# A hand-ordered attention-and-mixer kernel with another order table: the prologue's loads reordered, two loads assumed to land later, fewer repeated score matmuls

## The chip, the cores and the metric

One core of a Trainium2 chip. The metric is device time of one execution in microseconds (us). The kernel before took 784.28, 784.71 and 784.94 us in three runs, median 784.71. The execution that was profiled took 784.66 us; 782.9 us of it is the span from the first to the last instruction of the program, so 1.8 us lie around it. On this kernel a measurement can tell about 0.2% (1.57 us) from no change.

## The reference

```python
xn = _layernorm(x)                      # x: 1 x 2048 x 640, bf16
q, k, v = heads(xn @ wqkv)              # 32 heads of 20
s = softmax(q @ k.T * 20**-0.5) @ v @ wo
h = gelu(_layernorm(xn) @ w1)           # its four quarters shifted along the sequence by +1, -1, +2, -2
x1 = xn + shifted(h) @ w2
g = silu(x1 + gelu(_layernorm(x1) @ w3) @ w4)
return x + s * g
```

## The kernel before

The attention is done in eight quads of four heads (`attn_quad`, L1374), each quad in four chunks of 512 queries (`qc`), each chunk in 16 key tiles of 128 keys. For one key tile the four heads' scores are four tiles of 128 keys by 512 queries, each in one PSUM bank. ACT takes two heads at once through exp (`exp_act`, L1692, 128 x 1024); in some key tiles it takes all four at once (L1669, 128 x 2048). For another part of the key tiles DVE turns scores into integer bits (L1714) and DVE or POOL add offsets to them (L1602, L1600), which stands for the exp. PE then multiplies by the values (L1432 for ACT's tiles, L1614 for the bits). The number of exps on ACT is fixed by a table of how many blocks go to DVE (`ND`), which the change doesn't touch.

PE makes a score in one of two ways (`score_pair`, L1625). In **row mode** (L1623) one matmul with a contraction of 32 rows makes one head's tile, and four heads stand beside each other in the four row groups of the array. In **column mode** (L1640) four matmuls over all 128 rows and 32 columns each make one tile, from a masked copy of the queries (`QM`). All other products, the projections (`mm_tile`, L733) and the value products too, are in column mode. Whether a score runs in row mode is decided from the order alone (L252): it does if PE is in row mode already, or if the next PE task is a score too. A run of row-mode tasks between two column-mode tasks is called a burst here. `AGAIN` (L585) names score tiles whose matmul is issued once or more again, to the same result.

The second branch (`b_branch`) is woven between the quads: w1 with quad 0, w2 with quad 1, w3 and w4 with quads 2 to 5. `stack` (L1279) projects queries and keys of six heads at a time, `v_load` and `v_proj` (L1335, L1344) the values of half the heads; the second half's weights are loaded with quad 1 (`ld_wv1`). `b_w4` (L2101) loads half of w4 four times (L2110). The prologue loads x in eight pieces (L920), the first query and key weights (`ld_wp_0`, `ld_wp_1`, L1102) and the first value weights (`ld_wv0`, L1341), normalises x on DVE, ACT and POOL (L944 to L1028), transposes it on PE (L1079, evicted at L1087 and L1090), and makes the first keys and queries (`KT_0`, `QT_0`); chunk 0 of quad 0 starts with an early bound (`she`, L1192, `qade`, L1196). The end is a chain of output projections (`finish_qc`, `last_half`), in which half chunks of scores are made in pairs (L1489 in row mode, L1493 in column mode).

**Nothing here is scheduled while it runs.** `program` lists 6939 tasks with what they read and write. `TABLE` (L2138), a string, names every task once, two characters each, and behind a task that takes PSUM banks or probability buffers one character for each choice of them. `follow` (L219) walks it: the order in the string is the order on each engine, and the characters fix the banks. It also reckons start times with assumed durations (L302 to L305: a DMA is taken to land after its issue, 2050 ns, its bytes at 330 a ns, and `dlat`); these times emit no instruction. `plan_sync` (L323) adds the semaphore waits that the tasks need. So PE, ACT, DVE, POOL and the DMA issues on SP each run a fixed list in order, and a task whose operand is late holds all that stand behind it.

PSUM has seven banks for scores and projections and one for the value sums. A score can only be made when the last reader of its banks is done: the exp two or three places ahead of it on ACT, or a DVE eviction.

Of the kernel before, what the change touches and what calls it, by code (L numbers as in the profile page):

```python
# [477 lines left out]
class Cfg:  # L478
# [5 lines left out]
    def __init__(self, S=2048, D=640, H=32, F=1536):  # L484
# [100 lines left out]
        self.AGAIN = {(7, 1, 2, 0): 1, (7, 1, 4, 0): 2, (7, 1, 4, 2): 2, (7, 1, 4, 3): 2, (7, 1, 6, 0): 1, (7, 1, 6, 1): 2, (7, 1, 6, 2): 1, (7, 1, 9, 0): 1, (7, 1, 9, 1): 1, (7, 1, 9, 3): 1, (7, 2, 2, 2): 4, (7, 2, 2, 3): 1}  # L585
# [71 lines left out]
class Gen:  # L657
# [677 lines left out]
    def v_load(self, hf):  # L1335
        cfg = self.cfg
        D = cfg.D
        Wv = self.alloc(f"Wv{hf}", [cfg.KC, D // 2], BF16)
        src = self.aps["A_wqkv"].rearrange("(kc p) n -> p kc n", p=128)
        c0 = 2 * D + hf * (D // 2)  # L1340
        self.T("sp", C_SP, lambda e: e.dma_start(Wv[:, :, :], src[:, :, c0:c0 + D // 2]), writes=[self.A(f"Wv{hf}")], is_dma=True,  # L1341
               nbytes=128 * D * cfg.KC, name=f"ld_wv{hf}")
# [758 lines left out]
    def b_w4(self, n0, n1):  # L2101
        cfg = self.cfg
        T, A = self.T, self.A
        D, FC = cfg.D, cfg.FC
# [3 lines left out]
        for hh in range(2):  # L2108
            hs = slice(hh * HALF, (hh + 1) * HALF)
            T("sp", C_SP, lambda e, hs=hs: e.dma_start(W4[:, :, :], w4src[:, :, hs]),  # L2110
              writes=[A("W4")], is_dma=True, nbytes=FC * 128 * D, dlat=800.0, name=f"ld_w4_{n0 // 4}_{hh}", stream="w4")
# [27 lines left out]
    r"#Z$K#6#9#:#;#<#=#>#?#@&R###%$?#w#&$4#(#,#-$S#$#A#B#C#D#E#)#F#G#H#I#J#K$L#[#]#^#a#'#*#l#_#2#L#+#.&S#e#f#c#g#h#n#p#i$T$U#`#q#m#j$N#r$V$J#o$M#k$O#s#{#t#y$P%o#M#"  # L2139
    r"N#O#P$v'#x#Q#R#|$q%#z$Q$R#u#}${(#v$W#~$#$(#S#T$|$`$}$r$)$+$Y$X$*%$#$s$t$l&#b&Q#d$~$m$w$$$Z$n$o$u$p%#%%%&%'$x#U#V%($y$,$z$[$'$]#W#X#Y%`)%a$a$%$^$5$9$_%b#/&T#%"  # L2140
    r"g&%c%d%h$-$6$.%i%e$&$b$A$C%n$8$7$/$0$2$3&U&V%)$%j%8'&j(%.%&k%k%9%=)%>$:%?%@&l%/%*%+%0%,#0%1&m%:&n%;%A&W&X%2&c)&d%l$@$D&e%3%%4&f&g%<%f%5%6&['&]%C&^&_%q$;&o&Y$"
    r"E%-%7&`%r$$1%t#%u&w(%v&x%m$c$d$B&a%s$<&y&z&{$F$=&h$G&|$>$f$e$I$g*<$*?(*;#*@)%w'()')'**=%'+&6(',&7&8&9*9$*A)'-%B%D*8#*:#&})&:&~*4(*5)%E'#'$*6&'%**#*+$*,$$h(H%"
    r"x$H$i*>%K$&;$j%Z('&%U%%V$k%p%L%F)%y%W%[%G%H%]%^%I%M%X%z#5%N#4%_%P&(K%{'%|%}%Q%R%S%~*C'%J%O%Y*1(*2)*B&*D#%T*3(#7&#&&&&'&(&)&*';#'<'='>(G&$'?&+&-&.&<(I'@*.%&%*"
    r"-&&H$&2%&I&3&J&K&L*7*`'*_(*K$*/%&,*J#*I%&M*H&*0&?$&@&A*a&&B&4#&C*M*N*L$&D&5+'#+($*R(+)%*P%*O&*E'/#'0&q$*S(*U*F'1'2'3*X$*W#'4*Y#&=%&>&r&s*Q'*[&*T*Z%&t*V&u*b(+"
    r"3$(L+2#&v(J*i'*c)&Z&0*])*h&+4$'A*G'I('J'K'L*l'M*^3$*k+T+$$+%#*d('N+&)*o'*m%*n&*r*p('5$*s'6'7'8'9':*e+6#&E*v*q#(P+5$'B#+*+7&*f&+C(*g%*j)+D)'C'D'E'F'O&'U''V'W'"
# [135 lines left out]
```

## Time and profile before

| | us |
|---|---|
| median of three runs | 784.71 |
| profiled execution, whole | 784.66 |
| its span | 782.9 |
| PE, ACT, DVE, POOL busy | 771.1, 764.3, 700.4, 440.7 |
| exps of 128 x 1024 on ACT: count, summed busy time | 730, 677.1 |
| score matmuls in row mode: count | 1907 |
| score matmuls in column mode: count | 384 |

A line of the timeline reads: start in us, duration in us, engine, line of the kernel, operation, what is written <- what is read, how many were merged, and in brackets the idle time of the engine before it and what ended that. An instruction's end includes the time in which its pipeline drains, and the next one of the same engine starts inside it: in an unbroken run the exps start about 0.9 us apart, though one is shown as 1.02 us or longer.

### The profile page before, as it was taken

Reading aid. Unit: us, or ns where it says so; the run is one execution under the profiler, and the core shown is the slowest. Engines: PE = TensorE matmul, PEld = TensorE weight load, DVE = VectorE, ACT = ScalarE, POOL = GpSimd, SP = SyncE. Lnnn points to the kernel's source line nnn. Section 1 sums busy time; section 2 is a strip of 40 time slices with the busy share of each in tenths; the row PEclk is TensorE's granted clock in tenths of the full one; section 3 lists DMA queues with packets and bytes.
Section 4 is the critical chain, followed back from the end, with each engine's and each line's share of the span. In section 5 each row is a group of like instructions: output and inputs, shape, how many; then the busy total and the mean of one; then the engine's idle time right before and its main releaser. Section 6 shows DMA issues by size and latency. Waiting matters only on the chain.

```text
span 782.9 us, 28034 instructions
## 1 busy us (share of the span) xinstructions
PE 771.1 (98%) x12501; PEld 294.9 (38%) x12501; DVE 700.4 (89%) x1170; ACT 764.3 (98%) x803; POOL 440.7 (56%) x238
## 2 busy tenths in 40 slices
PE   8999999999999999999999999999999999999997
PEld 4433333335434322333433344333235333333554
DVE  7889899988999999997989889998989888898886
ACT  7999999999999999999999999999999999999996
POOL 5676646545257656566554654666454555636743
PEclk9999999999999999999999999999999999999999
DMA  5333442423131323623223341234431133114433
GB/s 173 34 111 76 108 110 67 102 79 70 28 72 21 57 66 72 134 55 66 46 62 74 67 93 35 65 59 85 103 70 23 32 55 81 19 19 136 106 119 120
DMA packets 141352, 58.12 MB, mean 74 GB/s; under 512 B 113728, under 2 KB 136432, under 8 KB 141232
## 3 DMA queue, kind: packets, MB, share of 16 engines
q1 hardware_dynamic: 141232, 56.33, 31.6%
q8 instruction: 98, 1.61, 0.9%
q14 instruction: 22, 0.18, 0.1%
HBM read 34.70 MB, written 10.33 MB: 58 GB/s over the span
## 4 chain that ended last, share of the span: by engine, by line
PE 59%; ACT 38%; DVE 1%; SPq 1%; DMA 1%; issue 0%
ACT arena L1692 33%; PE psum L733 22%; PE psum L1623 16%; PE psum L1614 9%; PE psum L1432 7%; ACT arena L2095 3%; PE psum L1640 2%; ACT arena L1669 1%; DMA arena<-in_A_wqkv_dram 1%; ACT arena L2123 1%; SPq L920 1%; PE psum L1489 1%; PE psum L1463 0%; PE psum L1493 0%; ACT L1692 0%; ACT L2095 0%
## 5 line engine op out<-in xcount | busy, mean ns | idle before, releaser
L1692 ACT ACTIVATE arena<-psum 128x1024 bf16<-128x1024 f32 x730 | 677.1, 1105 | 6.2 <-PE psum L1623 3.7
L1600 POOL TENSOR_TENSOR arena<-arena 128x2048 int32<-128x2048 int32 x92 | 330.2, 3598 | 197.1 <-DVE arena L1602 88.7
L1714 DVE TENSOR_SCALAR arena<-psum 128x512 uint16<-128x512 f32 x528 | 341.5, 683 | 39.1 <-PE psum L1623 31.1
L733 PE MATMUL psum<-arena 128*32 128x320 bf16 (+1 forms) x5808 | 335.0, 333 | 0.5 <-DMA arena<-in_A_wqkv_dram 0.5
L1623 PE MATMUL psum<-arena 32*128 32x512 bf16 x1907 | 252.3, 384 | 3.0 <-ACT arena L1692 1.8
L1614 PE MATMUL psum<-arena 128*22 128x512 bf16 x2112 | 183.6, 381 | 0.0
L733 PEld LDWEIGHTS psum<-arena 128*32 128x32 bf16 x5808 | 137.9, 96 | 120.6 <-issue 48.2
L1623 PEld LDWEIGHTS psum<-arena 32*128 32x128 bf16 x1907 | 69.0, 91 | 221.7 <-ACT arena L1692 114.4
L1432 PE MATMUL psum<-arena 128*22 128x512 bf16 x1456 | 139.3, 382 | 0.1
L1602 DVE TENSOR_SCALAR arena<-arena 128x4096 uint16<-128x4096 uint16 (+1 forms) x121 | 131.9, 1106 | 1.6 <-PE psum L1614 0.6
L1746 POOL TENSOR_TENSOR arena<-arena 128x512 bf16<-128x512 f32 x30 | 40.6, 1354 | 55.3 <-DVE arena L1602 41.9
L1614 PEld LDWEIGHTS psum<-arena 128*22 128x22 bf16 x2112 | 47.1, 90 | 60.7 <-issue 42.8
L1432 PEld LDWEIGHTS psum<-arena 128*22 128x22 bf16 x1456 | 35.5, 90 | 45.7 <-issue 31.2
L1640 PE MATMUL psum<-arena 128*32 128x512 bf16 x384 | 37.6, 382 | 0.0
L2088 DVE CAST arena<-psum 128x512 bf16<-128x512 f32 x48 | 32.7, 682 | 3.5 <-PE psum L733 3.3
L1299 DVE CAST arena<-psum 128x512 bf16<-128x512 f32 x40 | 27.2, 683 | 6.0 <-PE psum L733 5.7
L1911 POOL TENSOR_TENSOR arena<-arena 128x640 bf16<-128x640 bf16 x12 | 16.7, 1399 | 19.4 <-DVE arena L1845 11.1
L1669 ACT ACTIVATE arena<-psum 128x2048 bf16<-128x2048 f32 x13 | 25.2, 1941 | 0.5 <-PE psum L1623 0.5
L944 DVE BATCH_NORM_STATS2 arena<-arena 128x6 f32<-128x320 bf16 x54 | 24.1, 476 | 1.3 <-DMA arena<-in_A_x_dram 1.1
L1845 DVE SCALAR_TENSOR_TENSOR arena<-psum,arena 128x320 bf16<-128x320 f32 x32 | 15.6, 489 | 8.1 <-PE psum L733 7.7
L1733 DVE STREAM_TRANSPOSE arena<-psum 128x512 f32<-128x512 f32 x30 | 21.3, 710 | 1.2 <-PE psum L1432 0.8
L2095 ACT ACTIVATE arena<-arena 128x6144 bf16<-128x6144 bf16 x4 | 21.1, 5316 | 0.0
(135 smaller groups left out, 331.6 us busy)
## 6 DMA issues: line engine op xcount, KB each, us to landing
arena<-in_B_w_dram SPq DMA_DIRECT2D x48, 160.0 KB, 2.7
arena<-arena SPq DMA_DIRECT2D x124, 32.0 KB, 1.9
arena<-in_B_w_dram SPq DMA_DIRECT2D x4, 960.0 KB, 5.4
arena<-in_A_x_dram SPq DMA_DIRECT2D x8, 320.0 KB, 6.4
arena<-in_A_x_dram SPq DMA_DIRECT2D x16, 160.0 KB, 2.5
out_dram<-arena SPq DMA_DIRECT2D x16, 160.0 KB, 2.3
heads<-arena SPq DMA_DIRECT2D x120, 20.0 KB, 2.0
arena<-queries SPq DMA_DIRECT2D x28, 80.0 KB
```

The source lines that it names most:

```text
L733: ins = e.matmul(pb[32 * c:32 * c + 32, 0:N], lhsT(k, c), rhs(k, c), start=(k == 0), stop=(stop and k == nk - 1), tile_position=(0, 32 * c))
L1432: ins = e.matmul(pb[32 * i:32 * i + 22, 0:512], VA[:, ql, kts[i // 2], i, :], PT[:, slots[i // 2][0].slot, slots[i // 2][0].at(i % 2):slot ...
L1600: return e.tensor_tensor(dst.bitcast(I32), U[:, ub, 0:w].bitcast(I32), bass.AP(c.tensor, c.offset, [list(c.ap[0]), [0, w // 2]]), op=ALU.add)
L1602: fa if onp else lambda e, v=v, dst=dst: e.tensor_scalar(dst, U[:, ub, 0:w], EXP_B[v], None, op0=ALU.add),
L1614: ins = e.matmul(pb[32 * i:32 * i + 22, 0:512], wv, dst[:, at:at + 512].bitcast(BF16), start=first, stop=final, tile_position=(0, 32 * i))
L1623: return e.matmul(out, self.KT[32 * i:32 * i + 32, b, 128 * kt:128 * kt + 128], q, start=True, stop=True, tile_position=(32 * i, 0))
L1640: ins = e.matmul(out[32 * c:32 * c + 32, :], self.KT[:, b, 128 * kt + 32 * c:128 * kt + 32 * c + 32], self.QM[:, gb, i, :], start=True, st ...
L1669: lambda e: e.activation(self.PT[:, hp[0].slot:hp[0].slot + 2, :], self.psum[:, 512 * h0.slot:512 * h0.slot + 2048].rearrange("p (a b) -> ...
L1692: lambda e: e.activation(self.PT[:, hp.slot, :].rearrange("p (a b) -> p a b", b=512), self.banks(hs), AF.Exp, scale=cfg.scale),
L1714: T("dve", c_dve(512), lambda e, h=h, y=y: e.tensor_scalar(U[:, ub, y:y + 512], self.bank(h.slot)[:, :], a_exp, EXP_BIAS, op0=ALU.mult, op ...
L1746: return e.tensor_tensor(OnT.rearrange("p (k d a) -> p a k d", k=4, a=4), Ob[:, :].rearrange("p (a k d) -> p a k d", a=4, k=4), in1, op=AL ...
L2095: T("act", c_act(FC * 512), lambda e, G=G, i=i: e.activation(G[:, i, :, :], G[:, i, :, :], AF.Gelu_apprx_tanh), reads=gta, writes=gta, nam ...
```

## The change

- **TABLE** is another string: the same 6939 tasks in another order with other banks. Read task by task, ACT keeps 704 of 786 tasks at their place and moves none by more than 4; PE keeps 805 of 4466 and moves some by up to 123; DVE keeps 300 of 1170, POOL 104 of 234, SP 82 of 283.
- **AGAIN** goes from 12 tiles with 19 extra matmuls (all in chunks 1 and 2 of the last quad) to 5 tiles with 6 (one of them in quad 3).
- **dlat**, the assumed extra time to landing, goes from 800 to 2000 ns for w4 and from 0 to 1200 ns for the second value weights. These enter only the planner's arithmetic.

The prologue's loads are issued in this order (the number is the first x tile of a piece of two):

```
before: x0 x2 x4 x6 x12 x8 wp_1 x10 x14 wv0 wp_0
after:  x0 x2 x4 x6 x10 wp_1 x8 x14 x12 wp_0 wv0
```

Of ACT's list up to the first exp, both hold the same 23 tasks; the eviction of the first queries (`qev_0`) changes place with a Square pass over x (`ln1a_14_sxx14`) that stood behind it. On PE, `KT_0_0` comes ahead of the first `QT_0`, and one more task, `KT_1_3`, stands before the first burst.

Counted over both orders:

| | before | after |
|---|---|---|
| row-mode bursts on PE | 567 | 581 |
| summed depth of the bursts (matmuls of the fullest row group, repeats included) | 655 | 665 |
| score tiles in column mode (four 512-column matmuls each) | 96 | 82 |
| half-chunk pairs in column mode (16 matmuls each) | 6 | 8 |
| exps that take a bank freed by the exp right ahead of them | 2 | 2 |

The two of the last row are, before, the wide exp of key tile 8 in chunk 3 of quad 2 and an exp of key tile 6 in chunk 1 of quad 5; after, an exp of key tile 4 in chunk 0 of quad 1 and one of key tile 12 in chunk 2 of quad 7. Besides, an exp of the prologue (`exp0_0_3_1`) gets its banks from the eviction right ahead of it.

```diff
-        self.AGAIN = {(7, 1, 2, 0): 1, (7, 1, 4, 0): 2, (7, 1, 4, 2): 2, (7, 1, 4, 3): 2, (7, 1, 6, 0): 1, (7, 1, 6, 1): 2, (7, 1, 6, 2): 1, (7, 1, 9, 0): 1, (7, 1, 9, 1): 1, (7, 1, 9, 3): 1, (7, 2, 2, 2): 4, (7, 2, 2, 3): 1}
+        self.AGAIN = {(3, 1, 10, 2): 1, (7, 1, 2, 1): 1, (7, 1, 6, 2): 1, (7, 1, 12, 1): 2, (7, 1, 15, 0): 1}
...
-               nbytes=128 * D * cfg.KC, name=f"ld_wv{hf}")
+               nbytes=128 * D * cfg.KC, dlat=1200.0 * hf, name=f"ld_wv{hf}")
...
-              writes=[A("W4")], is_dma=True, nbytes=FC * 128 * D, dlat=800.0, name=f"ld_w4_{n0 // 4}_{hh}", stream="w4")
+              writes=[A("W4")], is_dma=True, nbytes=FC * 128 * D, dlat=2000.0, name=f"ld_w4_{n0 // 4}_{hh}", stream="w4")
...
 TABLE = (
...
```

More of the change, by code (lines that the diff above doesn't have):

```diff
@@ L2142 @@
[L2142 to L2145, printed above, removed]
@@ new lines @@
+    r"#&w)%C$0$@&o$B%u%v%w&x&y&Y$c$E%s$1$<$?$F$>&h&z%m&{*?#$d*<)&|*;(*@$*A%%x'(($G')*='%B'*$e$='+',&6)&7*9#*8$$f$I$g*:&$h'-&8&9&}($H*5(*4)&~*6(%E%D&:'#**#*+$'$'%$i"
+    r"$j%U%$k*,$%y%F$%V%G%H%W%o&;%K)%z(H*>%L'&%M%P(%Q%N%I%Z&%O%[%X%R%]%^%{'%|%S%J%}*C)%T%Y*B(%_*2&*1'%~&#(I&&(&'&(&)&<&*'d*D)*-(*3&&$&+*.)*/'&-#0';&'<'=&.'>'?&H#&I"
+    r"&2)&J&K(G(J&L*7*0&,'@&3&%*_&*`%*a$*J$*K#*H(&M*I)*L'*M&?#&@&A*N(L#4'A3$&B&C&4(&D*Q&+'$(K&5+(#*E*P(*T*O)&=(*F'/)&N+)&&>'0'1*S#&q#*W#*X$'2'3*Y(&r&s*R%*[(*Z)&t&u"
+    r"*V'4*U*])&v+2$+3#*h%*i&*l+4#*k*b(*c)'I#'J'K'L'M*G*d%'N+%#+$$*^*o&*n'*p%+&'*m(*s'5$'6'7'8'9*q)'.+5$*r+6#+T'e+7(&/':*e+**g&+C(*f%+D'*j$'U$'V'W'X'B&+E%'C'D'Y'E'"
@@ new lines @@
+    r"F+<%+=&'O''P'Q'R'S+.'+/(&E*v'G+9#+#'Z']$+>&'T+:$+X&+0'+W%+;$+8'^'_+Z+,'++('`'a*x+_#+K%+[+`$+J&+-#+?'b+c&F$+H(#7+G'+1*u+V$+b+L)+U%+o&&G&O&*w,+)*y+I$(P+n'+r'''"
+    r"H*|,*(+Y#*t*{,,(&P+M+q,.&+u$,-%+x,/&+v#+y+|*z+A'+^(+])*~*},K$+@&,J%+a)'f&'g,#+B$'h'i'j+h('l$+F'k,L'+i''m'n+N,:&+j%+f$&0,;%,>+e#'o+d,=+s(+t''p'q+g$,0,A%,D,9#,"
+    r"8$,B&,E+k+w)'r$+m(,<&+l'+p(+O-.'s't,@%,G$,H#,I$,?&&i'u'v'w+P'x#'y,C%'z'{'|'},N$,O#,W(,Z,X),P#+~,M(Q,w&,x%&p,&,),`',R$,_(,[,Q#,F'c#8'[3%+Q05(M$,c,y',b(N,p&,s%"
+    r",S)'~,q'+z+{,t$->)-?(,',r&,u(-@$+},T,e,(,~&-2#-#%-1$(#,5',$-5-4,v,%,i-$#,4((%$(&(',]&,6&,1#,2$,^%,f((()(+#(,,3),a((-(.,{#(*-8(,z$-;,7,g-&%-%&(O(R-9),k-<,|%,d"
@@ new lines @@
+    r"-H(-K,U#,V$-'&,l,}(/(0-G)-J,Y)-0&-/%-3%-(($,h-M(-L'-N#-O$-R,j,o,n-P#-k%-j&(1$-Q-U(2-6'-l)-E$-7(-F#.`(Y(a-:((3(4-I',m-)(7((5(8(6-A(-B'(9-=-p&-C&-g#.%)-s-h$(:("
+    r";-_.$((<-i%-X-*.&#-D(Z#-x&-c$(=-w%+R-[-d#-{-z-e$([(](^-u)06-v((_(`-y&-m.1&-q%-~#-}$-W-V-t.((.2'.)).#)-Z(S(.4.*%-a$.5-`#(T(U.+'.8(.;-b'.9).,&.'(V.<(v(W(X.?-n$"
+    r"-o#.-(-f-]/8'-r)/9&./(.0).3'(>../:((w((x(y.7#.6$.:%-Y&1(z-T({-^.I&.>+S.B-S.M#.L$(|.J#(@-|&b.H(?(.N)(A(B.A.D.d(.S'.E.T&.U'.c).=.K.g.P%.O$.Q$0I&.f0J.j(.m.V'.k)"
+    r".W&0K.X%.n0L0M.h%.i$.l&.b(.@0N.y&.|/k'/n.a).R.Y.G.q#(E.p$.z%.}.F-+/$&.e#(C(D.s(/%'/(.r).t).C.u'/'.Z07(08.~#/#$09.w'/E(/F)/H/&%/I.x&0:0;.{$0<)(-,(}(F/*.o/5#/6"
```

200 lines of the change are left out of this document (96 added, 104 removed).

## The prediction, as it stood before the result

> **What bounds the kernel now.** I read the page first: busy shares, the chain that ended last, the costliest groups.
>
> ```profile
> PE 771.1 (98%) x12501; PEld 294.9 (38%) x12501; DVE 700.4 (89%) x1170; ACT 764.3 (98%) x803; POOL 440.7 (56%) x238
> ...
> PE 59%; ACT 38%; DVE 1%; SPq 1%; DMA 1%; issue 0%
> ...
> L1692 ACT ACTIVATE arena<-psum 128x1024 bf16<-128x1024 f32 x730 | 677.1, 1105 | 6.2 <-PE psum L1623 3.7
> L733 PE MATMUL psum<-arena 128*32 128x320 bf16 (+1 forms) x5808 | 335.0, 333 | 0.5 <-DMA arena<-in_A_wqkv_dram 0.5
> ```
>
> PE and ACT are both full, and the chain goes back and forth between them. ACT's work is fixed (730 exps and the rest), so the time can only fall by ACT's idle 782.9 - 764.3 = 18.6 us, and by gaps too short for that count. The stretches show where it lies.
>
> ```profile
> 0.00:20.00 20.00, 17.21 (x408) 9.77 (x412) 15.88 (x65) 14.62 (x29) 11.62 (x37) 1.00 0.64 173
> 20.00:40.00 20.00, 19.99 (x407) 9.06 (x398) 17.18 (x44) 18.86 (x26) 12.58 (x18) 1.00 0.21 30
> 740.00:760.00 20.00, 19.93 (x454) 10.74 (x449) 17.41 (x30) 18.80 (x21) 9.39 (x6) 1.00 0.50 152
> 760.00:783.00 23.00, 17.05 (x476) 10.99 (x468) 16.87 (x33) 15.96 (x18) 8.34 (x6) 0.92 0.35 110
> ```
>
> The columns are the stretch, its length, then busy time of PE, weight loads, DVE, ACT, POOL, the granted clock, DMA. ACT is idle 5.4 + 1.1 us in the first 40 us and 1.2 + 7.0 us in the last 43, in all 14.7 of 18.6; the 700 us between hold 3.9. PE looks full, but its score weight loads mostly wait for a bank:
>
> ```profile
> PEld psum L1623 <- ACT arena L1692: 114.4, 304, 0.7
> ```
>
> So 304 of 567 bursts start when ACT frees a bank, after 0.38 us on average. The middle is a tight loop: ACT frees a bank, PE makes the next score, ACT takes it.
>
> **The longer landings: nothing.** The group of L733 above says that projections on PE idled 0.5 us in all, for one cause, wqkv in the prologue. The loads of w4:
>
> ```profile
> L2110 SPq DMA_DIRECT2D arena<-in_B_w_dram x4: 383/408/527, 401.4 to 648.5; - x4
> its engine sat idle before it (us, times) until:
> who waited for it (us, times):
> busy tenths in 40 slices 0000000000000000000000000000000000000000
> DMA to landing us min/median/max: 5.2/5.4/6.0
> ```
>
> The planner assumed 480 + 2050 + 983040 bytes/330 + 800 ns = 6.3 us from issue, and they landed in 5.2 to 6.0; nobody waited for one. The new 7.5 us only keeps users of w4 further behind. Value taken: 0; bounds 0 to -0.3 (a wait of the size of the 0.5 us above that another execution may hold).
>
> **The prologue: -0.35 us.**
>
> ```profile
> 6.41 1.41 SPq L1341
> 7.81 0.04 issue
> 7.86 6.11 DMA arena<-in_A_wqkv_dram
> 13.96 0.14 issue
> 14.10 2.32 PE psum L733 x44
> ```
>
> This is the chain that ended last, at its start: SP issues `ld_wv0` (1.41 us), then `ld_wp_0`, whose landing at 13.96 lets PE begin `QT_0`. The change puts `ld_wp_0` ahead, so it is issued some 1.4 us earlier (the wv0 issue is what stands between). The next limit is close:
>
> ```profile
> 12.76 0.82 PE L907 MATMUL psum<-arena 128*32 128x512 bf16 x12
> 14.10 0.83 PE L733 MATMUL psum<-arena 128*32 128x512 bf16 x12 [0.52 <-DMA arena<-in_A_wqkv_dram]
> ```
>
> And ACT's own line in the same stretch:
>
> ```profile
> 11.96 1.63 ACT L1087 ACTIVATE arena<-psum 128x512 bf16<-128x512 bf16 x3
> ...
> 16.40 0.72 ACT L992 ACTIVATE arena<-arena 128x640 bf16<-128x640 bf16 x1
> ...
> 17.63 2.62 ACT L1087 ACTIVATE arena<-psum 128x512 bf16<-128x512 bf16 x5 [0.41 <-PE psum L1079]
> ...
> 22.40 1.92 ACT L1692 ACTIVATE arena<-psum 128x1024 bf16<-128x1024 f32 x2
> ...
> 29.27 1.02 ACT L1692 ACTIVATE arena<-psum 128x1024 bf16<-128x1024 f32 x1 [0.74 <-PE psum L1623]
> ```
>
> The warm-up matmuls end at 13.58 and ACT's three evictions of transposed x at 13.59, so PE can start 0.5 us earlier, no more. One more task (`KT_1_3`, 0.21 us) then stands ahead of the first scores: 0.5 - 0.2 = 0.3. ACT does the same 23 tasks before its first exp (22.40) and can save at most the 0.41 us gap at 17.63 and some tenths at its other waits. I take -0.35. Bounds: -0.7 (gap and 0.3 of PE), and +0.1, because `qev_0` now waits behind a 0.72 us Square pass, and the bound that the first scores need hangs on it; this is the cost if the earlier PE doesn't cover it. Wv0 lands later by its neighbour's issue, and its first users move back in PE's list too: 0.
>
> **PE's work: +2.9 us, of which 0.8 shows.** Two places of PE's timeline and one group of instructions give the prices.
>
> ```profile
> 511.24 0.60 PE L733 MATMUL psum<-arena 128*32 128x512 bf16 x8
> 511.67 0.39 PE L1432 MATMUL psum<-arena 128*22 128x512 bf16 x4
> 511.99 0.61 PE L1623 MATMUL psum<-arena 32*128 32x512 bf16 x6
> 512.53 0.40 PE L1614 MATMUL psum<-arena 128*22 128x512 bf16 x4
> ...
> 24.01 0.39 PE L1623 MATMUL psum<-arena 32*128 32x512 bf16 x2
> 24.33 0.67 PE L733 MATMUL psum<-arena 128*32 128x320 bf16 x12
> ```
>
> ```profile
> L1493 PE MATMUL psum<-arena 128*32 128x256 bf16 x96 | 3.7, 273 | 0.0
> ```
>
> Two column tasks of 512 columns take 511.67 - 511.24 = 0.43, so 0.215 each. The same kind of task ahead of a burst takes 511.99 - 511.67 = 0.32: entering costs 0.105. A burst one deep lasts 24.33 - 24.01 = 0.32, two deep 512.53 - 511.99 = 0.54: about 0.215 for each depth and 0.105 for leaving. A half-chunk pair in column mode is 3.7/6 = 0.62, less the 0.18 by which a shown end outlasts the start of the next (0.40 - 0.215): 0.44. From the counts in the section on the change: 14 more bursts x 0.21 = +2.9; 10 more of depth x 0.215 = +2.1 (13 fewer repeats are in it); 14 fewer column scores x 0.215 = -3.0; 2 more column pairs x 0.44 = +0.9. Sum +2.9 us. The Trainium skill, page "TensorEngine Tiling (Array Packing)", section Key Properties, says that changing the tiling mode drains TensorE; this trace agrees, with 0.105 us at each edge, and by that rule alone, with no wait to hide them, the 28 further changes of mode cost all their 2.9 us.
>
> What hides it: the wait for a bank. Of 567 bursts 304 (54%) wait 0.38 us for ACT, more than a burst's 0.21 overhead, so 46% of 2.9 = 1.35 is uncovered; and PE carries 59% of the chain: 0.8. Bounds: 0 (all in waits) to +2.9 (all on the chain).
>
> **Banks: -1.1 us.** Where an exp takes the bank of the exp right ahead of it, ACT must stand still while PE makes the score. Before there are two such exps, at 298.12 and 512.51.
>
> ```profile
> 293.78 3.84 ACT L1692 ACTIVATE arena<-psum 128x1024 bf16<-128x1024 f32 x4
> 298.12 1.88 ACT L1669 ACTIVATE arena<-psum 128x2048 bf16<-128x2048 f32 x1 [0.50 <-PE psum L1623]
> ...
> 512.51 1.94 ACT L1692 ACTIVATE arena<-psum 128x1024 bf16<-128x1024 f32 x2 [0.59 <-PE psum L1623]
> ...
> 118.38 2.98 ACT L1692 ACTIVATE arena<-psum 128x1024 bf16<-128x1024 f32 x3 [0.36 <-PE psum L1623]
> ...
> 746.25 5.08 ACT L1692 ACTIVATE arena<-psum 128x1024 bf16<-128x1024 f32 x5 [0.55 <-PE psum L1489]
> ```
>
> One exp takes 1.02 (the row of 29.27), two in a row 1.94, so they overlap by 0.1, and each stall costs its idle time plus 0.1: 0.6 + 0.7 = 1.3 us. Both exps get banks freed earlier in the new order. The new order has two others, but where ACT stood still already: behind the wide exp at 116 (now 0.36 + 0.1; a full stall of 0.65 adds 0.2) and at 746 (0.55 + 0.1; adds nothing). The prologue's exp behind an eviction stands still now too (0.74 at 29.27). Net -1.1; bounds -1.3 and, if PE is late there for other reasons, 0. The other stalls of the middle have an exp's width of slack in both orders, and the number of such exps is alike; new ones I can't see, and I give them 0 with +-1.0, a bit less than the two just priced.
>
> **The end: 0.** Behind the score of key tile 2 in the last quad's third chunk 3 fewer bursts follow (-0.6), 2 more column pairs (+0.9), and about 0.3 us of column tasks moved ahead of it: 0, bounds +-0.5. Behind the pair at 762.6 the list is the same but for its inner order, so the last 20 us stay. The pairs are part of the +2.9 and not added again. The repeats that go are counted in the depth.
>
> **Sum.** 784.66 (the profiled execution) - 0.35 + 0.8 - 1.1 = 784.0; it stands 0.05 under the median of the runs, so the median is forecast at **784.0**, -0.1%.
>
> **The rivals.**
> - *Late bursts (slower).* The 14 further bursts stand where PE, not ACT, is late; each delays an exp that ACT can't make up, since it has no spare time in the middle (3.9 us idle in 700). Price: all 2.9 on the chain and the banks' gain lost to PE being late there too: 784.66 - 0.35 + 2.9 = 787.2. It decides once more than half of 2.9 (1.57 us) is on the chain with no gain from banks. For it: PE carries 59% of the chain. Against it: 304 waits for ACT. The Trainium skill's rule of the drain (page "TensorEngine Tiling (Array Packing)", section Key Properties) would give this one too.
> - *Covered (faster).* All 2.9 us fall in the 114 us of waits, and prologue and banks give their whole: 784.66 - 0.7 - 1.3 = 782.7; with stalls of the middle falling out well (-1.0) 781.7. Taken at 782.4. For it: the two stalls are plain in the trace.
> - *The change doesn't do what it says.* Nobody waits for w4 or wv1 now, the prologue's gain is lost at `qev_0`, and the rest cancels: 784.7.
>
> **How the numbers follow.** Forecast 0.36, no effect 0.08, covered 0.31, late bursts 0.25. The forecast's own range is 783.2 to 786.2: the terms' bounds partly cancel. Same (within 0.2%): 0.36 + 0.08 = 0.44; faster 0.31, slower 0.25; 0.2% is about what a measurement of this kernel can tell from no change. The range reaches to 781.2 and 788.0: below, the covered case with the middle's 1.0 and the tail's 0.5 (784.66 - 0.7 - 1.3 - 1.0 - 0.5 = 781.2); above, the late bursts with the middle's 1.0 of new stalls (787.2 + 1.0 = 788.2, less a little). About 1 in 10 is left out on each side.
>
> **What would show it.** Right: in the prologue PE starts L733 near 13.6 with no wait for in_A_wqkv, and the first exp near 22.05; no ACT gap of over 0.4 us at the old places 298 and 512; ACT idle in the middle within 1 us of 3.9; 1908 row-mode and 328 column-mode score matmuls; PE idle or waiting less by some 2 us while the span hardly moves. Wrong: waits on w4, ACT gaps before L1623 bursts in new places with more than 2 us in all, or a first exp later than 22.5.

## The result, and the profile after

| | before | after |
|---|---|---|
| median, 7 runs each on one chip (us) | 784.70 (784.28 to 784.94) | 781.94 (781.32 to 782.75) |
| ratio of after to before | | 0.9967, 95% interval 0.9956 to 0.9979 |
| profiled execution, whole (its span) | 784.66 (782.9) | 782.75 (780.9) |

After is faster by 2.76 us or 0.33%, more than the 0.2% that can be told from no change. The forecast was 784.0 and no difference. That did not come: the median lies below the forecast's own range (783.2 to 786.2), inside the wide one (781.2 to 788.0) and near the time of the rival "covered" (782.4). The profiled execution of after is the slowest of its seven, 0.8 us above their median, so its trace shows 1.9 us of the 2.8; most of the rest is in the prologue, which differs from one execution to the next (below).

The page of after, its rows for the engines, the chain that ended last and the groups of the exps, the projections and the two kinds of score:

```profile
PE 770.5 (99%) x12470; PEld 291.4 (37%) x12470; DVE 698.9 (89%) x1170; ACT 763.0 (98%) x803; POOL 441.4 (57%) x238
...
PE 57%; ACT 40%; DVE 1%; DMA 1%; issue 0%; POOL 0%; SPq 0%
...
L1692 ACT ACTIVATE arena<-psum 128x1024 bf16<-128x1024 f32 x730 | 676.7, 1106 | 6.6 <-PE psum L1623 4.0
...
L733 PE MATMUL psum<-arena 128*32 128x320 bf16 (+1 forms) x5808 | 331.6, 333 | 0.8 <-POOL arena L1911 0.7
L1623 PE MATMUL psum<-arena 32*128 32x512 bf16 x1908 | 254.3, 384 | 1.6 <-ACT arena L1692 0.6
...
L1640 PE MATMUL psum<-arena 128*32 128x512 bf16 x328 | 32.1, 381 | 0.0
```

The same engines are full and the chain goes on between the same two. The only wait of L733's matmuls that was left before, for a DMA of wqkv, is gone; 0.7 us for GpSimd has come. The score weight loads wait for a bank freed by an exp as often and as long, though there are 14 more bursts:

```profile
PEld psum L1623 <- ACT arena L1692: 113.3, 304, 0.7
```

The first two and the last two stretches of after (columns as before):

```profile
0.00:20.00 20.00, 17.97 (x420) 9.54 (x424) 16.37 (x67) 15.18 (x30) 11.92 (x37) 1.00 0.59 174
20.00:40.00 20.00, 19.93 (x410) 8.90 (x406) 17.73 (x44) 18.82 (x26) 12.32 (x16) 1.00 0.23 36
740.00:760.00 20.00, 19.33 (x468) 10.91 (x460) 17.68 (x28) 17.94 (x20) 8.89 (x5) 1.00 0.42 121
760.00:781.00 21.00, 15.10 (x452) 10.50 (x440) 13.43 (x30) 13.85 (x15) 6.99 (x5) 0.95 0.32 106
```

ACT is busy 0.56 us more in the first 20 us than before, and 0.86 us less from 740 to 760 (17.94 against 18.80). Those are a gain and a loss at the two ends, and both have a plain cause in the traces. Between 40 and 740 us ACT's idle time fell from 3.9 to 2.7 us (17.9 us in all, less 6.0 and 9.2 at the ends).

**How the lead grows.** ACT's list holds 786 tasks in nearly the same order in both kernels, so the start of its n-th task in the one, less that in the other, is the lead at that place. The waits for the activation table are rows that stand by themselves in ACT's timeline and make good milestones; the last row is the last eviction of the kernel. Before:

```profile
183.13 1.28 ACT L2003 ACT_TABLE_LOAD   x1
...
378.59 1.28 ACT L2095 ACT_TABLE_LOAD   x1
...
587.49 1.28 ACT L2095 ACT_TABLE_LOAD   x1
...
778.71 0.70 ACT L1863 ACTIVATE arena<-psum 128x640 bf16<-128x640 f32 x1 [2.77 <-PE psum L1857]
```

After:

```profile
181.39 1.28 ACT L2003 ACT_TABLE_LOAD   x1
...
376.26 1.28 ACT L2095 ACT_TABLE_LOAD   x1
...
584.92 1.28 ACT L2095 ACT_TABLE_LOAD   x1
...
776.70 0.70 ACT L1863 ACTIVATE arena<-psum 128x640 bf16<-128x640 f32 x1 [2.78 <-PE psum L1857]
```

So after leads by 1.74, 2.33, 2.57 and 2.01 us. Task by task the lead is 0.53 us at the first exp, 0.97 at 42 us, 0.84 at 49 us, and then it grows in steps: 0.5 around 123 us, 0.4 at 168, 0.6 from 290 to 378. It is 2.48 at 498 us, 2.78 at 750 us, and 0.7 is lost at 757. Steps of 0.1 to 0.2 us that go back again stand between, also where no exp has a gap in front of it, so a step of that size says little by itself.

**The prologue.** The chain of after at its start, and ACT there:

```profile
11.53 1.57 ACT arena L1087 x3
...
13.14 0.40 PE psum L733 x4
...
13.55 1.70 PE psum L733 x28
```

```profile
21.87 4.69 ACT L1692 ACTIVATE arena<-psum 128x1024 bf16<-128x1024 f32 x5
...
28.25 1.94 ACT L1692 ACTIVATE arena<-psum 128x1024 bf16<-128x1024 f32 x2 [0.55 <-PE psum L1623]
```

PE starts the projections at 13.14 instead of 14.10, with the one key task `KT_0_0`, when ACT's third eviction is done (13.10); the queries follow at 13.55, as soon as their weights are there (landed at 13.51). The exp that stood at 29.27 before stands at 28.25.

**The stalls.** ACT's rows around the four places that the prediction priced:

```profile
115.16 1.93 ACT L1669 ACTIVATE arena<-psum 128x2048 bf16<-128x2048 f32 x1
117.64 7.51 ACT L1692 ACTIVATE arena<-psum 128x1024 bf16<-128x1024 f32 x8 [0.55 <-PE psum L1623]
...
295.56 2.02 ACT L1669 ACTIVATE arena<-psum 128x2048 bf16<-128x2048 f32 x1
297.31 4.84 ACT L1692 ACTIVATE arena<-psum 128x1024 bf16<-128x1024 f32 x5
...
507.83 1.94 ACT L1692 ACTIVATE arena<-psum 128x1024 bf16<-128x1024 f32 x2 [0.26 <-PE psum L1623]
510.02 4.69 ACT L1692 ACTIVATE arena<-psum 128x1024 bf16<-128x1024 f32 x5 [0.25 <-PE psum L1623]
...
757.10 5.61 ACT L1692 ACTIVATE arena<-psum 128x1024 bf16<-128x1024 f32 x6 [1.28 <-PE psum L1489]
```

The wide exp of 298 has no gap in front of it any more. Behind the wide exp at 115 the gap is 0.55 where it was 0.36, as the prediction had it, but the eight exps behind it run without a break, while before had another gap four exps later (0.48). Before, that exp and PE's burst for it:

```profile
122.75 3.77 ACT L1692 ACTIVATE arena<-psum 128x1024 bf16<-128x1024 f32 x4 [0.48 <-PE psum L1623]
...
122.11 0.60 PE L1623 MATMUL psum<-arena 32*128 32x512 bf16 x6
```

After, the bursts that make the same scores:

```profile
120.80 0.40 PE L1623 MATMUL psum<-arena 32*128 32x512 bf16 x4
...
121.67 0.39 PE L1623 MATMUL psum<-arena 32*128 32x512 bf16 x2
```

The orders tell what was changed. Before, the burst is two deep, and one of the two scores that the exp needs (`exp1_0_6_0`) stands in its row group behind a score for VectorE. After, that exp and the next one (`exp1_0_7_1`) change places, the scores come in two bursts one deep each, and both exps start without a gap (121.29 and 122.21).

At 510 a gap of 0.59 became 0.25, but gaps of 0.19 and 0.26 ahead of it (500 and 508 us) are new, and the lead is 2.48 at 498 us and 2.49 behind the four. The gap at 757 is 1.28 where the same exp had 0.46 before (759.06).

### The profile page after: what moved, and what is told of

The parts are those of the page before. It is cut to its first block, busy times and chain, and to the rows that moved or that the text cites. A ratio compares the mean times of both kernels' runs of the same rounds, so it can differ in the third digit from the quotient of the medians.

```text
span 780.9 us, 27979 instructions
## 1 busy us (share of the span) xinstructions
PE 770.5 (99%) x12470; PEld 291.4 (37%) x12470; DVE 698.9 (89%) x1170; ACT 763.0 (98%) x803; POOL 441.4 (57%) x238
## 4 chain that ended last, share of the span: by engine, by line
PE 57%; ACT 40%; DVE 1%; DMA 1%; issue 0%; POOL 0%; SPq 0%
ACT arena L1692 35%; PE psum L733 21%; PE psum L1623 16%; PE psum L1614 10%; PE psum L1432 7%; PE psum L1640 1%; ACT arena L2095 1%; ACT arena L1669 1%; ACT arena L2003 1%; DMA arena<-in_A_x_dram 1%; ACT arena L2123 1%; PE psum L1489 1%; PE psum L1463 1%; PE psum L1493 0%; ACT L1692 0%; PE psum L1079 0%
## 5 line engine op out<-in xcount | busy, mean ns | idle before, releaser
L733 PE MATMUL psum<-arena 128*32 128x320 bf16 (+1 forms) x5808 | 331.6, 333 | 0.8 <-POOL arena L1911 0.7
L733 PEld LDWEIGHTS psum<-arena 128*32 128x32 bf16 x5808 | 135.6, 96 | 121.1 <-issue 48.6
L1602 DVE TENSOR_SCALAR arena<-arena 128x4096 uint16<-128x4096 uint16 (+1 forms) x121 | 130.3, 1091 | 2.6 <-PE psum L1614 1.2
L1640 PE MATMUL psum<-arena 128*32 128x512 bf16 x328 | 32.1, 381 | 0.0
L1733 DVE STREAM_TRANSPOSE arena<-psum 128x512 f32<-128x512 f32 x30 | 21.3, 710 | 2.1 <-PE psum L1623 0.9
L2117 DVE TENSOR_TENSOR arena<-psum,arena 128x320 bf16<-128x320 f32 x32 | 15.6, 486 | 6.8 <-PE psum L733 6.6
```

Of the source, the lines that this page charges most:

```text
L733: ins = e.matmul(pb[32 * c:32 * c + 32, 0:N], lhsT(k, c), rhs(k, c), start=(k == 0), stop=(stop and k == nk - 1), tile_position=(0, 32 * c))
L1602: fa if onp else lambda e, v=v, dst=dst: e.tensor_scalar(dst, U[:, ub, 0:w], EXP_B[v], None, op0=ALU.add),
L1640: ins = e.matmul(out[32 * c:32 * c + 32, :], self.KT[:, b, 128 * kt + 32 * c:128 * kt + 32 * c + 32], self.QM[:, gb, i, :], start=True, st ...
```

## The experiments

The order string can be cut where the same set of tasks is done in both kernels and the same PSUM banks are held; before's part on one side and after's part on the other then make a legal third order, called a graft below (where only the buffers of the exps differ at the cut, they are renamed on one side). The cuts lie at about 49, 264, 498 and 730 us. All leads below are by ACT's tasks in one profiled execution against the profile of before, given at before's times. Each median stands beside that of before on the same chip.

**The whole prologue, first cut.**

```diff
 TABLE
-    before's order up to 49 us
+    after's order up to 49 us
     before's order from 49 us
```

> Before, with the order of after up to a seam at about 49 us (loads, prologue, first scores, and what follows them), and before's own order and banks from there on. Theory (the gain is a sum of local gains of order and banks): all of the prologue's gain stays, about 0.9 us, so 783.8 us where before stands at 784.7, and ACT runs 0.8 to 1.0 us ahead from 45 us to the end. Rival (the waits behind the seam eat it): 784.4 to 784.7, with the lead gone by about 125 us. Rival (the prologue is the whole gain and the rest only keeps it): 781.9.

796.53 us (before 785.07), ratio 1.0140 (1.0126 to 1.0155). Neither theory: ACT stands still for 12 us, and SyncE's and the chain's rows say for what.

```profile
60.10 1.02 ACT L1692 ACTIVATE arena<-psum 128x1024 bf16<-128x1024 f32 x1 [11.88 <-PE psum L1623]
```

```profile
SPq L1390 <- POOL arena L1410: 30.1, 1, 30.1
```

```profile
50.37 3.46 POOL arena L1410
...
53.85 0.64 SPq L1390
...
55.78 1.88 DMA arena<-arena
```

Read backwards: the exp waits for a score, the score for DMAs of L1390 that SyncE issues at 53.85, SyncE for a memset of GpSimd (L1410). The memset is late because the planner ties each GpSimd task to the last task of VectorE ahead of it *in the string* that takes the lock which the two share there (`lock`, L255). At the cut 19 GpSimd tasks and loads had come to stand behind VectorE's last tasks of the first part. It is a fault of the cut, no part of the change, but it prices a late GpSimd task: ACT goes from 1.0 us ahead at 42 us to 11.7 behind by 100 us, and stays 11.7 behind to 750 us.

**The old prologue in after.**

```diff
 TABLE
-    after's order up to 49 us
+    before's order up to 49 us
     after's order from 49 us
```

> After, with the order of before up to the seam at about 49 us. Theory (sum of local gains): after less the prologue's share, 782.8 to 783.0 us where after stands at 781.9. Rival (the prologue's gain is eaten by later waits): 781.9 to 782.2. Rival (the prologue is all): 784.7.

796.55 us, ratio 1.0143 (1.0130 to 1.0156): the same fault, an ACT stall of 10.8 us at 49 us, so nothing on the change.

**Fewer repeats alone.**

```diff
-        self.AGAIN = {(7, 1, 2, 0): 1, (7, 1, 4, 0): 2, (7, 1, 4, 2): 2, (7, 1, 4, 3): 2, ...
+        self.AGAIN = {(3, 1, 10, 2): 1, (7, 1, 2, 1): 1, (7, 1, 6, 2): 1, (7, 1, 12, 1): 2, (7, 1, 15, 0): 1}
```

> Before, its tables as they are, with only after's list of repeated score tiles: 10 repeats fewer, 2.2 us less of score matmuls by 0.215 us each. Theory (PE's work lies in its waits for ACT, so less of it is worth nothing): 784.5 to 784.7 us. Rival (fewer repeats are where the gain comes from): 782.0 to 782.5. If the share of PE in the chain decides (59 per cent): 783.4.

785.62 us (before 785.07), ratio 1.0006 (0.9996 to 1.0017). The expectation miscounted: the lists hold 19 and 6 extra matmuls, so 13 fewer are left, 2.8 us of PE's work; one entry is in both, so 18 go and 5 come. By the clock it is worth nothing, and the trace tells the two kinds apart. The 18 that go, all in the last quad, win ACT nothing: PE stands idle in their place (0.33 us for ACT at 716.87). The ones that come cost: ACT is 0.14 us ahead up to 334 us, where the repeat in quad 3 stands, and 0.06 behind from there; two column-mode repeats at 719 us put a gap of 0.23 in front of the next exp, and past 720 us ACT is 0.29 behind. The change's gain does not come from them.

**More repeats in the middle.** One score tile in a one-deep burst of each chunk of the quads 0 to 6 but the first is made twice (before's list, and 27 entries more):

```diff
+        (0, 1, 11, 2): 1, (0, 2, 11, 1): 1, (0, 3, 5, 2): 1, (1, 0, 14, 0): 1, (1, 1, 5, 1): 1, ...
```

> Before, with 27 score tiles more computed twice, one in a one-deep burst of each chunk of the quads 0 to 6: 27 x 0.215 = 5.8 us more of score matmuls, and not an instruction in another place. Hidden altogether: 784.7 us. The price that my prediction took (0.8 shown of 2.9, 27 per cent): 786.3. By PE's share of the chain (59 per cent): 788.1. All shown: 790.5.

788.57 us (before 785.07), ratio 1.0045 (1.0032 to 1.0058): 3.5 us of 5.8 or 60% (by the interval 43 to 78%), near what PE's share of the chain says (788.1) and more than twice what the prediction reckoned (786.3). The profile agrees by another way: the prologue of that execution was late by 2.6 us, and between 42 us and the end ACT falls back by 3.1 us more, 53%, in one step of 0.7 us near 268 us, steps of 0.1 to 0.2 us at other places and none at many of the 27.

**The prologue with the cut mended.** As the first kernel, but GpSimd's 19 tasks and loads behind the cut stand as early beside VectorE's tasks as in the kernel that they are from.

> Before, with the order of after up to a seam at about 49 us and before's own order and banks from there on. It is the first prologue kernel again with its seam mended: GpSimd's 19 instructions and loads that stood behind the seam stand again at their old places beside VectorE's, so that the 11 us stall at 47 us goes. Theory (the gain is a sum of local gains): the prologue's 0.9 us stay, ratio to before 0.9988, ACT 0.8 to 1.0 us ahead from 45 us to the end. Rival (waits behind the seam eat it): ratio 0.9996 to 1, the lead gone by about 125 us. Rival (the prologue is the whole gain): 0.9967.

783.54 us (before 784.78), ratio 0.9981 (0.9972 to 0.9990): 1.24 us. The milestones of its ACT:

```profile
181.87 1.28 ACT L2003 ACT_TABLE_LOAD   x1
...
377.33 1.28 ACT L2095 ACT_TABLE_LOAD   x1
...
586.22 1.28 ACT L2095 ACT_TABLE_LOAD   x1
...
777.46 0.70 ACT L1863 ACTIVATE arena<-psum 128x640 bf16<-128x640 f32 x1 [2.77 <-PE psum L1857]
```

A lead of 1.26, 1.26, 1.27 and 1.25 us: what the first 49 us win is still there at the end, within 0.02 us, and the medians differ by 1.24. The rival that later waits eat it is refuted; the rival that the prologue is all, as well.

**The old prologue in after, mended in the same way.**

> After, with the order of before up to the seam at about 49 us, mended in the same way. Theory (sum of local gains): after less the prologue's share, ratio to before 0.9979, ACT level with before at 45 us and 1.8 us ahead at 740 us. Rival (the prologue's gain is eaten later): 0.9967. Rival (the prologue is all): 1.0.

791.63 us, ratio 1.0084 (1.0067 to 1.0102). The mending does not suffice here: ACT still stands 5.9 us at 50.6 us behind the same memset, which the chain shows released by VectorE at 46.8 us only; after's order puts it behind VectorE's task there, and before's prologue brings that later. So "after without its prologue" was not measured.

**The loads alone.** Only SyncE's order of the first fifteen issues:

```diff
-x0 x2 x4 x6 x12 x8 wp_1 x10 x14 wv0 wp_0
+x0 x2 x4 x6 x10 wp_1 x8 x14 x12 wp_0 wv0
```

> Before, with only SyncE's order of the first fifteen issues taken from after (wp_1 behind the tenth x tile, wp_0 and wv0 last); every other engine keeps its order. If the loads are the prologue's gain: the first KT projection starts at 13.6 us or before where before's first projection starts at 14.1, the first exp at 21.9 instead of 22.4, ratio 0.9990 to 0.9994. If the order of PE's instructions is needed as well: before's first projection is of QT and waits for wp_0, the last to land at 13.5 us, so first exp 22.3 to 22.9 and ratio 1.0 to 1.0006.

784.58 us (before 784.78), ratio 0.9995 (0.9986 to 1.0004): by medians -0.2 us, and not told from nothing. In its profiled execution, which was its fastest (784.11), PE starts the projections at 12.88 us, without a wait for the weights, the first exp is at 21.44, and ACT leads by 0.74 from 28 us to 750 us. In that execution the first x tiles were ready as early as in the mended kernel (ACT's sixth task 0.76 and 0.73 us ahead of before's profile); there the lead was 1.27. So, profile against profile, the loads gave 0.74 of 1.27 us with these landings, and the order of the tasks the other 0.5; but this profile is of its kernel's fastest execution. By the medians the loads gave 0.2 and the order of the tasks 1.0. How the prologue's gain divides between the two is not settled.

**After with before's end.**

```diff
 TABLE
     after's order up to 730 us
-    after's order from 730 us
+    before's order from 730 us, buffers of the exps dealt out anew
```

> After up to a seam at about 730 us, with before's order, banks and repeats from there on (the buffers of the exponentials are dealt out anew behind the seam). After's longest new stall, 1.47 us of ACT at 754.7 us, should be before's 0.66 again. Sum of local gains: 2.6 to 2.8 us ahead of before at 740 us and to the end, ratio 0.9966, level with after or up to 0.8 us faster. Rival (after's tail is part of its gain): 0.9975 to 0.998, slower than after by 0.6 to 1 us.

783.06 us (before 784.78), ratio 0.9972 (0.9962 to 0.9983): 1.7 us faster than before, where after is 2.8. The lead is 2.8 us up to 726 us, 2.2 from 730 us and 1.6 from 751 us to the end. The new stall did not show that after's end is bad as a whole; the graft lost more than it saved. Whether before's order or the buffers dealt out anew lost it stays open.

**After up to 264 us, before from there.**

> After up to a seam at about 264 us, before's order, banks and repeats from there on. Theory (local gains that add up, none of them eaten): ACT 1.8 us ahead of before at 264 us as in after, and just as far ahead at 770 us; ratio 0.9977. Rival (the gain of one stretch is lost in the waits of the next): the lead shrinks behind the seam to 0.9 us or less, ratio 0.999.

782.92 us (before 784.74), ratio 0.9977 (0.9967 to 0.9987): as the sum of local gains has it. ACT leads by 0.96 at 49 us, 1.96 at 262 us, and by these milestones to the end:

```profile
376.63 1.28 ACT L2095 ACT_TABLE_LOAD   x1
...
585.53 1.28 ACT L2095 ACT_TABLE_LOAD   x1
...
776.74 0.70 ACT L1863 ACTIVATE arena<-psum 128x640 bf16<-128x640 f32 x1 [2.77 <-PE psum L1857]
```

1.96, 1.96 and 1.97. So after's stretch from 49 to 264 us is worth 1.00 us, as it is in both profiles of after.

**After's order from 264 to 498 us alone, in before.**

> Before, with after's order and banks between two seams at about 264 and 498 us alone. In that stretch after gains 0.65 us on before, 0.6 of it at the stall of the wide exp at 298 us. Theory (local, additive): ACT level with before up to 264 us, 0.65 us ahead from 320 us to the end, ratio 0.9992. Rival (the gain needs what after does ahead of 264 us): 1.0.

784.34 us (before 784.74), ratio 0.9999 (0.9990 to 1.0007): too small for the clock, but the trace shows it. ACT is 0.57 us behind before up to 262 us (a late prologue), 0.17 us *ahead* at 301 us, and 0.16 behind again at 498; behind the cut it keeps 0.24 to 750 us. The gap at 298 is gone and gave 0.79 us, but other stalls took back 0.46. Net 0.41 at the second cut and 0.33 behind it. In after itself the same stretch gives 0.64, in both profiles. The difference arises at 355 us, where PE waits 0.17 us for a VectorE transpose (L1733) that it does not wait for in after, and ACT loses 0.28. So the theory of purely local gains holds here only in part.

**After's order from 498 us alone, in before.**

> Before up to a seam at about 498 us, and after's order, banks and repeats from there on. In that stretch after gains 0.4 us at 511 us and loses 0.8 at 754.7 us, and its end is 0.5 us worse than its lead at 740 us. Theory (local, additive): 0.3 us ahead of before at 740 us, 0.3 to 0.5 us behind at 770 us, ratio 1.0004 to 1.0006. Rival (after's tail is a gain, as the graft of before's tail at 730 us would have it): ratio 0.9990 to 0.9994.

784.17 us (before 784.74), ratio 0.9996 (0.9987 to 1.0005). The profile: 3.23 us behind at 498 us (a late prologue once more), 2.96 at 531, but 3.2 again from 545 to 700, 3.00 at 750 and 2.97 at the end. So after's order from 498 us on is worth 0.26 us here, in steps too small to place. The gap at 757 is only 0.47 us here (0.46 before, 1.28 after), and two rows per kernel tell why. After, GpSimd's timeline and the line of the loads of x for the residual (L1835; the last number is the time from issue to landing), issued at 750.41:

```profile
754.56 1.39 POOL L1911 TENSOR_TENSOR arena<-arena 128x640 bf16<-128x640 bf16 x1 [2.10 <-DVE arena L1740]
```

```profile
L1835 SPq DMA_DIRECT2D arena<-in_A_x_dram x1: 327/327/327, 750.4 to 750.4; - x1
...
DMA to landing us min/median/max: 4.0/4.0/4.0
```

After's end in before, issued at 756.19:

```profile
759.53 1.40 POOL L1911 TENSOR_TENSOR arena<-arena 128x640 bf16<-128x640 bf16 x1 [1.28 <-DVE arena L1539]
```

```profile
L1835 SPq DMA_DIRECT2D arena<-in_A_x_dram x1: 328/328/328, 756.2 to 756.2; - x1
...
DMA to landing us min/median/max: 3.2/3.2/3.2
```

The trace names VectorE as releaser, and two different lines of it, done 0.3 us and longer before. GpSimd started 0.12 and 0.13 us behind the landing (750.41 + 4.03 = 754.44, 756.19 + 3.22 = 759.40): what it waited for was the load. The load took 0.81 us longer in after, and the gap on ACT is 0.81 us longer. Between them stands PE, which waits for that GpSimd task ahead of the score that ACT needs:

```profile
756.01 0.73 PE L733 MATMUL psum<-arena 128*32 128x320 bf16 x16 [0.67 <-POOL arena L1911]
```

**After once more, unchanged.**

> After once more, unchanged, for a second profile and a second median. Its first profiled execution took 782.75 us, the slowest of its seven, and holds a stall of ACT of 1.47 us at 754.7 us; before with after's tail from 498 us on does not show that stall. If it belongs to that one execution: no stall over 0.8 us at that place, ACT 2.6 to 3.0 us ahead of before at 770 us as at 740 us, a profiled time of 781.7 to 782.2 us. If it belongs to after's order: a stall of 1.3 to 1.6 us there again, and 782.6 to 782.9 us. First exp at 21.4 to 21.9 us as in the other kernels with after's loads; ratio 0.9956 to 0.9979 as before.

781.96 us (before 784.92), ratio 0.9966 (0.9952 to 0.9980). Both expectations fail in part. (Their 1.47 us counts from start to start of the two exps, less the 0.9 us of an unbroken run; the row's gap is 1.28.) The stall is there again (a gap of 1.13 us, 1.32 by that count; the load took 3.9 us), so it is no accident of one execution, though its length follows the load's landing; yet the profiled execution took 781.96, because its prologue was 0.6 us earlier, with the first exp at 21.24 us, earlier than expected. The lead is 3.40 at 752 us and 2.79 at the end.

## Why the prediction was right or wrong

**The sum of the parts.** What ACT's lead gains in each stretch, by the two profiles of after and by the kernels that hold the stretch without the rest of after behind it (for the last three, without the rest ahead of it too):

| stretch (us) | after | after again | in a third order |
|---|---|---|---|
| to 49 | 0.84 | 1.47 | 1.27 (mended prologue) |
| 49 to 264 | 1.00 | 1.00 | 1.00 (after up to 264) |
| 264 to 498 | 0.64 | 0.64 | 0.41 |
| 498 to 750 | 0.30 | 0.29 | 0.23 |
| 750 to the end | -0.77 | -0.62 | 0.03 |
| sum | 2.01 | 2.79 | |

By the clock the first row is 1.24 and the first two together 1.82 (1.97 in that trace); the rows below them are read from traces alone. So the change has no one cause: it is a prologue that starts earlier and many small gains in the middle, and one loss at the end. Against the forecast's -0.65, of which -0.35 is prologue and -0.3 middle, the prologue gave 0.9 more (by the clock), the middle from 49 to 498 us 1.3 more, and the end took back 0.6 to 0.8 where nothing was reckoned.

- **What bounds the kernel:** right. PE and ACT by turns, the middle a tight loop, in which a lead won on ACT is kept (1.26 us for 600 us).
- **The longer landings, 0:** right. The two `dlat` values by themselves change no instruction of any engine, and nobody waits for a load of w4 or of the second value weights in either trace. The loads of w4 in after:

```profile
L2110 SPq DMA_DIRECT2D arena<-in_B_w_dram x4: 373/406/527, 398.9 to 644.8; - x4
its engine sat idle before it (us, times) until:
who waited for it (us, times):
...
DMA to landing us min/median/max: 5.2/5.5/5.7
```

- **The prologue, -0.35 (-0.7 to +0.1):** right about what stood in the way, the query weights, but too small by 0.9 and outside its bound of -0.7. It gave the new order of the tasks nothing or a cost; that order gave 0.5 us profile against profile, 1.0 by the medians. And "so PE can start 0.5 us earlier, no more" failed: the limits that it named, ACT's evictions at 13.59 and the warm-up matmuls at 13.58, moved too (13.10 and 13.07 in after), since they depend on when the x tiles land (the chain of after goes back to a DMA of x that lands at 8.10). And the limit was one draw of a wide lot:

| first projection / first exp (us) | |
|---|---|
| before's loads, seven profiles | 14.10 / 22.40, 13.85 / 22.14, 13.93 / 22.27, 14.68 / 22.98, 15.03 / 25.02, 15.11 / 23.41, 15.66 / 25.64 |
| after's loads, seven profiles | 13.14 / 21.87, 12.70 / 21.24, 12.88 / 21.44, 12.92 / 21.46, 13.20 / 21.73, 13.21 / 21.75, 13.26 / 21.79 |

  The two latest of the first row are from the slowest executions of their kernels (790.42 and 787.63 us), so the usual spread is smaller.

The latest of the first row is PE's row in the kernel with after's end:

```profile
15.66 1.94 PE L733 MATMUL psum<-arena 128*32 128x512 bf16 x25 [2.08 <-DVE arena L973]
```

  The trace names VectorE, but in all seven the first projection starts 0.13 to 0.14 us behind the landing of the query weights, whatever engine is named (in before 13.96 and 14.10, as the prediction's chain shows; here 15.53 and 15.66). Issued at 7.86 in before and at 7.9 here, they took 6.1 us to land there and 7.6 here. In before they are the last in the list, behind wv0, and set the start every time; in after they stand ahead of wv0, one key task that does not need them goes first, and in six of the seven they were there by 12.55, before PE came to them.
- **PE's work, +2.9 of which 0.8 shows:** the share was wrong. The prediction multiplied 46% (bursts that do not wait) by 59% (PE's share of the chain) to 27%. Repeats spread over the middle showed 60%, close to the chain's share by itself, which counts the hidden waits already. By it the 2.9 would have cost 1.7. That cost does not appear: the middle of after gains 1.64 us from 49 to 498 us. Nor do the new bursts hide in the wait that the prediction named, since 304 of them wait for an exp's bank in both kernels. At the exp of 122.75 us (above) one deep burst became two shallow ones, and there the further burst belongs to the gain; the prediction had priced bursts as cost alone. That is read at one place, and no run added bursts and nothing else, so what the 14 cost or win in all stays open.
- **Banks, -1.1:** right at 298, where the graft won 0.79, and at the new stall behind the wide exp at 116, which cost its 0.2 (0.55 for 0.36); the gap at 746 went from 0.55 to 0.64. Wrong at 511: the gap shrank by 0.34, but new ones just ahead of it took that back (lead 2.48 at 498, 2.49 behind it; in the graft 0.10 won). In the graft other stalls of the new order behind 298 took 0.46 back as well.
- **Other stalls of the middle, 0 +-1.0:** 0.5 at 123 us and 0.4 at 168 were not foreseen; with smaller steps they make up the 1.00 us of the stretch from 49 to 264 us, at the edge of the bounds.
- **The end, 0 +-0.5:** outside its bounds in after, which loses 0.77 and 0.62 us behind 750 us. A wait was missed: a load of the residual, issued when VectorE has freed its buffer, lands 4.0 and 3.9 us later and costs the 0.7 to 0.8 us at 757; in the graft it landed after 3.2 us, and nothing was lost. Loading it earlier was not tried.
- **The rivals:** "late bursts" (787.2) is refuted by the result (its mark of 1.57 us is 0.2% of the time; half of 2.9 would be 1.45); "covered" came nearest in time, but by a prologue larger than its 0.7 and gains in the middle, not by cover; that its time came near is luck. The forecast of "no difference" stood on the small prologue and on the 0.8.

No kernel of the study beat after.

## What to carry to other kernels

In a kernel with fixed orders and a full engine, follow that engine's n-th instruction through both traces: a step of more than some 0.2 us that does not go back is a stall won or lost, it stays to the end where the orders agree behind it, and the steps add up to the change in time. A term of the prologue rests on landings that vary from one execution to the next, so ask which load stands last in its queue and price its spread, not the one landing that the profile shows. And for extra work spread over the middle the chain's share of its engine was near the share that showed (59% and 60%), with nothing left to multiply it by; repeats in the last quad, where PE waited, showed nothing.

## What was not expected of the hardware

- The middle repeats itself almost exactly: two executions of different kernels with the same order keep their distance within 0.02 us over 600 us (1.26, 1.26, 1.27, 1.25), though their prologues differ by microseconds.
- The same query weights, issued at 7.86 and 7.9 us behind the same loads, landed after 6.1 us in one execution and 7.6 in another; the residual's 160 KB load took 3.2 to 4.0 us at the same place.
- A memset of GpSimd (L1410) that starts at 50.3 instead of 37.8 us stops ACT for 12 us, by way of SyncE's queue and four DMAs (L1390): an engine that is 56% busy can hold the whole kernel.
